# A first pass that gives way to the transform's steps at eight points of a unit instead of four

## The chip, the cores and the metric

The kernel runs on one core of a Trainium2 chip. The metric is the device time of one execution, in microseconds (us). All names of engines are those of the profile: PE is TensorE's matrix multiply, PEld its weight load, DVE is VectorE, ACT is ScalarE, POOL is GpSimd, and SP is SyncE, which here only issues DMAs.

## What is computed

Forward and backward of a gated mix of two branches over one sequence of S = 2048 rows of D = 1024, all in bf16:

```
g   = sigmoid(sum(A_x * gate_w))                       # one gate per row
a   = irfft2(rfft2(A_x) * (A_w_r + i A_w_i))           # spectral branch
b   = relu(A_x @ B_w1 + B_b1)**2 @ B_w2 + B_b2         # dense branch, F = 3584
out = g * a + (1 - g) * b
```

The outputs are `out` and the gradients of A_x, A_w_r, A_w_i, B_w1, B_b1, B_w2, B_b2 and gate_w for a given grad_out. The gradients are sums over rows or columns of products of the same sizes, and the spectral branch is transformed once more for grad_out.

## The kernel before

**Two streams of work.** The kernel has a main stream, the dense branch with its gradients, and a side stream, the spectral branch (a two-dimensional transform there, a product with the filter, and the transform back). Both are Python generators. `spread` (L1797) runs the main one, and at each of its `yield`s it adds a rate, times the weight that was yielded (none counts as 1.0), to what is due, and calls `next` on the side stream until as many side steps are done as are due.

**How the order comes about.** What is written is not yet the order on the engines. The framework's planner lays the instructions out on each engine when the kernel is built: with durations that it assumes, it always takes what is ready and was written first. Two kinds of edges hold it: real dependencies (data, and buffers that must come free), and edges that the kernel adds by hand to fix an order (`after`, `in_turn`, `behind`). `later["last"]` is the DVE instruction that ended the newest `back_`, `turn["PE"]` the newest matmul of the main stream.

**The main stream's first pass** is `mlp_in` (L770 to L1125). It makes the hidden layer and its gradient for 3584 features, in pairs of 128-feature chunks. After a start of its own it walks 23 units. A unit (class `Unit`, L921) is a 256-feature by 1024-row piece of the hidden layer, computed by seven products instead of eight (Strassen's scheme in the form of Winograd): p1, p5, p6, p7, p4, p3 and, for the unit after it, p2. Each is a chain of four 128x512 matmuls into one PSUM bank (L928). Between them run four `back_` calls for the unit before: eight 128x512 matmuls each into a bank `pd` (L827), and one DVE instruction that multiplies the bank by the hidden activations (L831, `dhT`).

- The banks of `ph` (p1, p6, p7 and p4 share X; p5 and p3 share V) are two; those of `pd` and `pZ` (p2) are two, together.
- p1, p6 and p7 leave partial sums, and ACT copies X out after each one (L935, tiles `cu`, `u2`, `cu`); the next chain on X may only start after the copy.
- `rest` adds the partial sums on DVE (L947), then ACT applies the bias and ReLU (L945, L948); `square` squares on ACT (L795) and stores to DRAM.

**The side stream** is `aside` (L1910). It has three stages of steps:

- `first_stage` (L743), four steps for each of 16 pairs of row tiles: pk0 and pk1 are eight 128x128 matmuls each (L293) and an ACT copy (L297); pu0 and pu1 are ten matmuls (L325) and three ACT copies (L303 to L307). pk1 also holds the six DVE instructions of `folds` (L272 to L284) for the next pair, pu1 two DVE additions (L312, L313) and three POOL-issued stores; pk0 issues loads on POOL (L741).
- `fft_mid` (L333), after eight steps of preparation, eight steps m.0 to m.7 for each of 16 groups m. m.0 is `spectra` (eight matmuls, L435), the gradient products of the half before, ACT copies (L443 to L445) and a load; m.1 is the other half's ACT copies and load; m.2 two DVE products (L453); m.3 `rows_of` (eight matmuls, L472), an ACT copy and loads and stores on POOL; m.4 a DVE sum (L458) and two DVE results (L488, L489); m.5 gradient products (L500, L501) and two DVE sums (L426); m.6 two more sums and two results; m.7 two products and a sum, POOL work and an ACT multiplication.
- `fft_out` (L591), which runs after the first pass.

All matmuls of the side stream write tiles of two banks each, named `ps2`, of which there are two. 11 side steps are done before the units begin; the rate then is 1.75 steps for a yield until `fft_mid` begins (`"mid" in later`), and 1.5 after that; in the last five calls of the pass it is 0.

**The points where the first pass gives way.** In the unit of before there are four: after p5, after the second `back_`, after the third, and after p2. The counter `left_` (L1926) is the number of yields of the pass, 100.

Of the kernel before, what the change touches and what calls it, by code (L numbers as in the profile page):

```python
# [141 lines left out]
def kernel(  # L142
# [30 lines left out]
    S2, DC, FC = g.S2, g.DC, g.FC  # L173
# [596 lines left out]
    def mlp_in():  # L770
# [52 lines left out]
        def grads(fc, sb, ss, rT, dhT):  # L823
            w_ = w2T[fc // FGC]
            pd = d_bank("pd")
            for ec in range(DC):
                turn["PE"] = mm(  # L827
                    pd[:], lhsT=w_[:, ec, fc % FGC * P : (fc % FGC + 1) * P], rhs=dbT[:, ec, ss],
                    start=(ec == 0), stop=(ec == DC - 1),
                )  # L830
            return STT(  # L831
                out=dhT, in0=pd[:], scalar=2.0, in1=rT, op0=ALU.mult, op1=ALU.mult,
                accum_out=gb1part[:, fc, sb : sb + 1],
            )

        def load_w2(fg, earlier=None, halves=(0, FGW // 2)):

            if fg not in w2T:
                w2T[fg] = wb.tile([P, DC, FGW], BF16, name="w2T", tag="w2T", bufs=2)
            for h in halves:  # L840
                f0 = fg * FGW + h
                after(turned(w2T[fg][:, :, h : h + FGW // 2], B_w2[f0 : f0 + FGW // 2, :]), earlier)
# [5 lines left out]
        def load_w1(fp):  # L848
            w1[fp] = f1.tile([P, DC, PW], BF16, name="w1f", tag="w1f") if fp == 2 else wb.tile([P, DC, PW], BF16, name="w1g", tag="w1g", bufs=2)
            ld(out=w1[fp][:], in_=w1v[:, :, fp * PW : (fp + 1) * PW])  # L850
# [6 lines left out]
        def store(scr, t_, fp, sp):  # L857
            cols2 = slice(2 * sp * SW, 2 * (sp + 1) * SW)
            st(out=scr[2 * fp : 2 * fp + 2, :, cols2].rearrange("c p s -> p c s"), in_=t_[:])  # L859
# [18 lines left out]
        def back_(fp, s, c):  # L878
            if (fp, s // 2) not in dh:
                dh[fp, s // 2], left_of[fp, s // 2] = wide("dhT"), 4  # L880
            last = grads(2 * fp + c, s, rows_(s), rTs.pop((fp, s, c)), dh[fp, s // 2][:, c, rows_(s % 2)])
            later["last"] = last
            left_of[fp, s // 2] -= 1
            if not left_of[fp, s // 2]:
                store(dhT_scr, dh.pop((fp, s // 2)), fp, s // 2)
# [23 lines left out]
        def w_sums(fp, tie=None):  # L909
            (a11, a12), (a21, a22) = w_quads(fp)  # L910
            if fp % 2:
                s_ = kept[:, NT - 2 : NT, :].rearrange("p t (n f) -> p (t n) f", f=P).rearrange("p (q n) f -> p q n f", q=4)
            else:
                s_ = wb.tile([P, 4, KH, P], FP16, name="Sw", tag="Sw", bufs=1)
            s1, s2, s3, s4 = (s_[:, n] for n in range(4))
            for out, x, y, op in ((s1, a21, a22, ALU.add), (s2, s1, a11, ALU.subtract), (s3, a11, a21, ALU.subtract), (s4, a12, s2, ALU.subtract)):
                after(V(out=out, in0=x, in1=y, op=op), later["last"] if tie else None, mybir.DependencyClass.NoSync)
                yield
            S_[fp] = {1: s1, 2: s2, 3: s3, 4: s4}
# [70 lines left out]
        def sum_of_db(n):  # L990
            ec, h = divmod(n, 2)
            summed = nc.vector.reduce_sum(out=gb2[:, ec, h : h + 1], in_=dbT[:, ec, h * S // 2 : (h + 1) * S // 2], axis=mybir.AxisListType.X)
            after(summed, later["last"], mybir.DependencyClass.NoSync)

        def grad_of_b2():
            whole = wb.tile([P, DC], BF16, name="gb2b", tag="gb2b")
            V(out=whole[:], in0=gb2[:, :, 0], in1=gb2[:, :, 1], op=ALU.add)
            pb = fps.tile([DC, P], BF16, name="pb2", tag="ps2", bufs=2)
            nc.tensor.transpose(pb[:], whole[:], identb[:])
            row = wb.tile([DC, P], BF16, name="gb2r", tag="gb2r")  # L1000
            nc.vector.tensor_copy(out=row[:], in_=pb[:])
            st(out=out_7.rearrange("(c p) -> c p", p=P), in_=row[:])
# [31 lines left out]
        def freed_rows(n, low, high):  # L1034
            if n == freed + 1:
                again(slice(2 * low, 2 * low + 2), later["last"])
            elif n == len(seq) - 1 and high:
                again(slice(6 + 2 * high, 8 + 2 * high))
# [6 lines left out]
        def one_due():  # L1045
            if due:
                fg_, h = due.pop(0)
                load_w2(fg_, later["last"], (h,))

        later["due"] = one_due  # L1050
        for n, u in enumerate(units_):
            fg, pr = divmod(u.fp, NPR)
            if (pr, u.sp) == (0, 0):
                one_due(), one_due()
            if (u.fp, u.sp) == (LAST - 2, 1):
                load_w1(LAST)
            elif u.sp == 0 and u.fp < LAST - 1:
                load_w1(u.fp + 1)
            u.p1()
            if n:  # L1060
                units_[n - 1].square(0, u.copy)
            back_(*waiting[0])
            u.p5()
            freed_rows(n, 0, 1)
            if first and u.sp and "mid" in later and u.fp >= FC // 4:
                turned_group(0, *first.pop(0), later["last"])
            yield
            next(more_sums, None)
            u.p6()
            freed_rows(n, 1, 2)  # L1070
            if n:
                units_[n - 1].square(1, u.copy)
            back_(*waiting[1])
            next(more_sums, None)
            follows = u.fp + 1 if u.sp == 1 and u.fp < LAST - 2 else {(LAST - 2, 0): LAST - 1, (LAST - 1, 1): LAST}.get((u.fp, u.sp))
            ahead_ = w_sums(follows, True) if follows else iter(())
            dealt = ahead_ if (u.fp, u.sp) != (LAST - 2, 0) else iter(())
            next(dealt, None)
            yield
            u.p7()  # L1080
            back_(*waiting[2])
            next(more_sums, None)
            next(dealt, None)
            freed_rows(n, 2, 0)
            yield
            back_(*waiting[3])
            for _ in ahead_:
                pass
            next(more_sums, None)
            if pr == 0 and u.sp == 0:  # L1090
                later["blocks"] = later["last"]
            if 0 < fg < FG - 1 and (pr, u.sp) == (0, 0):
                if "mid" in later:
                    due.extend((fg + 1, h) for h in (0, FGW // 2))
                elif fg < 3:
                    load_w2(fg + 1, later["last"])
                else:
                    late = fg + 1
            elif late and (pr, u.sp) == (0, 1):
                load_w2(late, later["last"])  # L1100
                late = None
            if 0 < n <= 2 * DC:
                sum_of_db(n - 1)
            elif n == 2 * DC + 1:
                grad_of_b2()
            u.p4()
            freed_rows(n, 3, 3)
            u.p3()
            if n + 1 < len(units_):
                units_[n + 1].p2()  # L1110
            yield
            waiting = [(u.fp, 2 * u.sp + j, c) for c, j in ((0, 0), (0, 1), (1, 1), (1, 0))]
        again(slice(NT - 2, NT))
        units_[-1].square(0), units_[-1].square(1)
# [15 lines left out]
    def turned_group(n, i, k, earlier):  # L1130
        scr, fg = (h2T_scr, dhT_scr)[n // FG], n % FG
        rows_ = scr[:].rearrange("c p s -> (c p) s")[fg * FGW + i * FGW // 2 : fg * FGW + (i + 1) * FGW // 2]
        tiles, f_ = slice(k * NT // 2, (k + 1) * NT // 2), slice(i * FGW // 2, (i + 1) * FGW // 2)
        after(turned(group(n)[:, tiles, f_], rows_[:, k * S // 2 : (k + 1) * S // 2]), earlier)
# [706 lines left out]
    warm(7)  # L1841

    units = mlp_in()
    rows_of_x(0, 2)
    vrow = f1.tile([FC + DC, P], BF16, name="vrow", tag="vrow")
# [74 lines left out]
    def counted():  # L1920
        for _ in side:
            count[0] += 1
            yield

    spec = counted()
    left_ = [8 * (FC // 2 - 2) + 4]  # L1926

    def first_rate():
        left_[0] -= 1
# [59 lines left out]
```

## Time and profile before

| | |
|---|---|
| median of 3 runs | 1193.3 us (1192.56 to 1193.49) |
| the profiled execution | 1191.93 us |
| its span, first to last instruction | 1190.2 us |
| PE busy | 1177.4 us (99%) |
| DVE busy | 895.3 us (75%) |
| ACT busy | 531.5 us (45%) |
| POOL busy | 387.6 us (33%) |
| granted PE clock | 1.00 |

The units of the first pass run from about 79 us to 430 us of the span. Stage one of the side stream lies beside units 0 to 7 (78 to 205 us), `fft_mid` beside units 8 to 22 and on into the next pass.

How to read it: a matmul's record lasts 379 ns for 128x512, but the next one starts about 216 ns after it, since matmuls are pipelined. So the busy share hides short stalls, and the start-to-start distances in the timeline tell more. Waits are put down to the semaphore that came last.

### The profile page before, as it was taken

What the parts mean: (1) busy time and instruction counts of PE and PEld (TensorE: products, weight loads), DVE (VectorE), ACT (ScalarE), POOL (GpSimd) and SP (SyncE); (2) the same over time, 40 slices, a digit from 0 to 9 for tenths busy, and PEclk for the clock granted to TensorE, in tenths of its full rate; (3) what the DMA queues carried; (4) which work ended last, traced back from release to release, by engine and by line L of the source; (5) the groups of instructions that cost most, each with busy time, mean ns of one, the idle gap of its engine ahead of it and who ended that gap; (6) DMA issues with size and microseconds to landing.
All of it is one profiled execution on the core that took longest, in us unless ns stands there. A gap on an engine that the chain in (4) does not pass through costs nothing.

```text
span 1190.2 us, 19485 instructions
## 1 busy us (share of the span) xinstructions
PE 1177.4 (99%) x7275; PEld 640.5 (54%) x7275; DVE 895.3 (75%) x1598; ACT 531.5 (45%) x961; POOL 387.6 (33%) x618
## 2 busy tenths in 40 slices
PE   8999999999999999999999999999999999999998
PEld 5555555444444444444447999998544444444444
DVE  6888887788989887877637666676785777976757
ACT  5678888577777772444324666564100010000000
POOL 0234433555858573755231233221001110000000
PEclk9999999999999999999999999999999999999999
DMA  9997585677969779888997999995799999564530
GB/s 251 298 291 235 166 215 170 199 211 179 249 169 232 239 241 186 195 192 212 225 200 157 232 229 260 234 217 153 251 193 228 263 287 282 170 199 147 181 125 36
DMA packets 329464, 249.84 MB, mean 210 GB/s; under 512 B 187912, under 2 KB 287658, under 8 KB 328858
## 3 DMA queue, kind: packets, MB, share of 16 engines
q1 hardware_dynamic: 268352, 112.12, 44.2%
q0 software_dynamic: 35136, 111.72, 29.9%
q10 hardware_dynamic: 25882, 24.76, 7.0%
q8 instruction: 57, 0.93, 0.3%
q14 instruction: 37, 0.30, 0.1%
HBM read 114.82 MB, written 89.67 MB: 172 GB/s over the span
## 4 chain that ended last, share of the span: by engine, by line
PE 78%; DVE 14%; ACT 3%; issue 2%; DMA 2%; SPq 1%; ACTq 0%; DVEq 0%
PE pX L1275 15%; PE xX L1576 14%; PE pV L1275 12%; PE pd L827 11%; PE xV L1576 7%; PE ph L928 6%; PE xZ L1576 4%; PE ph L820 2%; PE pui L325 1%; DVE dhT L831 1%; DVE rT L947 1%; PE pki L635 1%; DVE tt L453 1%; PE pu L325 1%; PE pZ L928 1%
## 5 line engine op out<-in xcount | busy, mean ns | idle before, releaser
L827 PE MATMUL pd<-dbT,w2T 128*128 128x512 bf16 x896 | 210.1, 379 | 3.4 <-DMA w2T<-in_B_w_dram 1.5
L827 PEld LDWEIGHTS <-w2T 128*128 128x128 bf16 x896 | 86.4, 98 | 107.6 <-issue 6.2
L1576 PEld LDWEIGHTS <-dS 128*128 128x128 f16 x686 | 66.4, 98 | 79.0 <-issue 3.4
L831 DVE SCALAR_TENSOR_TENSOR dhT<-pd,rT 128x512 bf16<-128x512 f32 x112 | 76.6, 684 | 33.7 <-PE pd L827 32.9
L1627 POOL DMA_DIRECT2D out_dram<-ot x32 | 17.4, 544 | 246.1 <-DVE ot L1683 128.0
L1693 ACT ACTIVATE w2br<-w2br,dsc 128x512 f32<-128x512 bf16 x8 | 5.8, 724 | 174.5 <-DVE ot L1683 117.4
L1576 PE MATMUL xX<-oT,dS 128*128 128x512 f16 x336 | 76.4, 379 | 0.6 <-DVE eR L1605 0.5
L1291 ACT COPY u<-pX 128x512 f32<-128x512 f32 x56 | 32.8, 586 | 90.5 <-PE pX L1275 84.9
L1576 PEld LDWEIGHTS <-odd 128*128 128x128 bf16 (+1 forms) x462 | 44.8, 98 | 51.5 <-issue 0.9
L1576 PEld LDWEIGHTS <-even 128*128 128x128 bf16 (+1 forms) x448 | 43.6, 98 | 52.6 <-issue 0.7
L1275 PEld LDWEIGHTS <-T 128*128 128x128 f16 x672 | 64.6, 98 | 7.5 <-issue 0.2
L948 ACT ACTIVATE rT<-rT 128x512 bf16<-128x512 bf16 x69 | 43.4, 629 | 42.3 <-DVE rT L947 41.8
L795 ACT ACTIVATE h2T<-rT 128x1024 bf16<-128x1024 bf16 x56 | 59.6, 1065 | 0.2
L1295 DVE TENSOR_TENSOR whi<-pV,u 128x512 bf16<-128x512 f32 x28 | 19.3, 689 | 47.1 <-ACT u L1291 47.0
L491 POOL DMA_DIRECT2D y_scr<-pc x64 | 47.2, 738 | 22.7 <-DVE pc L488 12.9
L1275 PEld LDWEIGHTS <-S 128*128 128x128 f16 x336 | 32.5, 98 | 40.8 <-DVE S L1207 1.9
L453 DVE TENSOR_TENSOR tt<-x,w 128x1028 f16<-128x1028 f16 (+1 forms) x64 | 41.9, 689 | 11.0 <-issue 5.8
L1275 PEld LDWEIGHTS <-resL 128*128 128x128 bf16 x448 | 43.1, 98 | 4.9
L1275 PEld LDWEIGHTS <-resR 128*128 128x128 f16 (+1 forms) x448 | 42.9, 98 | 4.9 <-issue 0.2
L1295 DVE TENSOR_TENSOR wlo<-pV,u 128x512 bf16<-128x512 f32 x28 | 19.2, 687 | 32.0 <-PE pV L1275 31.9
L859 POOL DMA_DIRECT2D h2T_scr<-h2T x28 | 20.9, 746 | 67.1 <-ACT f L285 30.2
L239 POOL DMA_DIRECT2D r<-y_scr x48 | 28.0, 588 | 42.4 <-ACT re L614 33.1
(382 smaller groups left out, 2803.7 us busy)
## 6 DMA issues: line engine op xcount, KB each, us to landing
h2T_scr<-h2T POOLq DMA_DIRECT2D x28, 512.0 KB, 4.2
dhT_scr<-dhT POOLq DMA_DIRECT2D x28, 512.0 KB, 5.2
y_scr<-pc POOLq DMA_DIRECT2D x64, 128.0 KB, 4.2
ax_scr<-yo POOLq DMA_DIRECT2D x16, 512.0 KB, 5.3
out_dram<-ot POOLq DMA_DIRECT2D x31, 256.0 KB, 3.3
z<-z_scr ACTq DMA_DIRECT2D x60, 128.0 KB, 3.4
out_dram<-whi POOLq DMA_DIRECT2D x28, 256.0 KB, 5.2
out_dram<-wlo POOLq DMA_DIRECT2D x28, 256.0 KB, 4.8
```

The lines of the kernel that those rows point to most:

```text
L239: st(out=a, in_=b) if stored else st(out=b, in_=a)
L453: V(out=tt[:, k, :, :, 0:W], in0=x[:, a : a + 2, :, 0:W], in1=by, op=ALU.mult)
L491: st(out=columns_of(y_scr, c, h), in_=pc[:, n])
L795: after(nc.scalar.activation(h2T, rT, ACT.Square), behind_, mybir.DependencyClass.NoSync)
L827: turn["PE"] = mm(pd[:], lhsT=w_[:, ec, fc % FGC * P : (fc % FGC + 1) * P], rhs=dbT[:, ec, ss], start=(ec == 0), stop=(ec == DC - 1),)
L831: return STT(out=dhT, in0=pd[:], scalar=2.0, in1=rT, op0=ALU.mult, op1=ALU.mult, accum_out=gb1part[:, fc, sb : sb + 1],)
L928: turn["PE"] = mm(acc[:], lhsT=lhs[:, t, :], rhs=rhs[:, t, :], start=start and t == 0, stop=t == KH - 1, skip_group_check=True,)
L948: nc.scalar.activation(rT, rT, ACT.Relu)
L1275: self.mm = mm(out, lhsT=lhs[:, t, m * P : (m + 1) * P], rhs=rhs[:, t, :], start=start and t + a == 0, stop=t == KH - 1, skip_group_check= ...
L1291: turn["ACT"] = nc.scalar.copy(out=t_[:], in_=self.X[:])
L1295: turn["DVE"] = self.added = V(out=self.half(row, j), in0=self.sums(acc), in1=self.sums(t_), op=ALU.add)
L1576: ins = mm(acc, lhsT=lhs[:, fc, :], rhs=rhs[:, fc, :], start=start and fc == 0, stop=fc == KH - 1 and bias is None, skip_group_check=True,)
```

## The change

The unit yields at eight points, each with weight 0.5, where it yielded at four with weight 1. The four old points stay; new ones come after p1, after p6, after p7, and after the fourth `back_` (ahead of p4).  The counter becomes 192, the number of yields of the pass now. No instruction is added or taken away, and no rate changes.

```diff
             u.p1()
             if n:
                 units_[n - 1].square(0, u.copy)
+            yield 0.5
             back_(*waiting[0])
             u.p5()
             freed_rows(n, 0, 1)
...
-            yield
+            yield 0.5
             next(more_sums, None)
             u.p6()
             freed_rows(n, 1, 2)
             if n:
                 units_[n - 1].square(1, u.copy)
+            yield 0.5
             back_(*waiting[1])
...
             next(dealt, None)
-            yield
+            yield 0.5
             u.p7()
+            yield 0.5
             back_(*waiting[2])
...
             freed_rows(n, 2, 0)
-            yield
+            yield 0.5
             back_(*waiting[3])
...
             elif n == 2 * DC + 1:
                 grad_of_b2()
+            yield 0.5
             u.p4()
             freed_rows(n, 3, 3)
             u.p3()
             if n + 1 < len(units_):
                 units_[n + 1].p2()
-            yield
+            yield 0.5
...
-    left_ = [8 * (FC // 2 - 2) + 4]
+    left_ = [16 * (FC // 2 - 2)]
```

Which side step is called where follows from `spread` by arithmetic. Steps of a unit are numbered in their order, in brackets:

```
stage one, units 0 to 6, seven steps a unit:
 before  p1 back0 p5 [1 2] p6 back1 [3 4] p7 back2 [5 6] back3 p4 p3 p2 [7]
 after   p1 [1] back0 p5 [2] p6 [3] back1 [4] p7 [5] back2 [6] back3 [7] p4 p3 p2
fft_mid, units 9 to 22, six steps a unit:
 before  p1 back0 p5 [A B] p6 back1 [C] p7 back2 [D E] back3 p4 p3 p2 [F]
 after   p1 [A] back0 p5 [B] p6 back1 [C] p7 [D] back2 [E] back3 p4 p3 p2 [F]
```

Since eight steps make a group and six make a unit, the steps that fall on A and D repeat every four units. A is m.1, m.7, m.5, m.3 in turn, and D is m.4, m.2, m.0, m.6. At the end of the pass 150.25 steps are due before and 150.125 after, so 151 are done either way.

## The prediction

> **What bounds the kernel now.** I read the page first, then the busy times of the stretches before, in and after the units' walk.
>
> ```profile
> span 1190.2 us, 19485 instructions
> ...
> PE 1177.4 (99%) x7275; PEld 640.5 (54%) x7275; DVE 895.3 (75%) x1598; ACT 531.5 (45%) x961; POOL 387.6 (33%) x618
> ```
>
> ```profile
> core 0: us, PE busy (x) PEld busy (x) DVE busy (x) ACT busy (x) POOL busy (x), PEclk, DMA share, GB/s
> 78.00:205.00 127.00, 126.12 (x898) 70.64 (x897) 105.12 (x228) 105.73 (x210) 50.39 (x92) 1.00 0.72 211
> 205.00:440.00 235.00, 233.16 (x1174) 100.63 (x1173) 204.78 (x446) 170.48 (x301) 153.31 (x236) 1.00 0.79 215
> ```
>
> PE is the bound, at a granted clock of 1.00. In stage one (78 to 205 us) DVE and ACT are each 83% busy, in `fft_mid` (205 to 440) DVE is at 87%. So PE sets the time, and the others can only make it stall. Next the waits of PE from 78 to 440 us, all of them, and the longest of DVE and of ACT:
>
> ```profile
> PE pd L827 <- DVE dhT L831: 1.5, 3, 0.7
> PE ph L928 <- ACT u L935: 0.4, 2, 0.2
> PE pk L293 <- ACT u L307: 0.2, 1, 0.2
> ```
>
> ```profile
> DVE dhT L831 <- PE pd L827: 17.7, 13, 3.6
> ...
> ACT rT L948 <- DVE rT L947: 41.8, 42, 2.8
> ```
>
> These rows show only idle time, and a pipelined record hides a short stall. So I took the distances from one matmul's start to the next in the timeline. A 128x512 matmul is followed after 216 ns (median), a 128x128 one after 56, and going into or out of `px` and `pv` costs 95 to 99 more. Beyond these medians there are 16 stalls of over 0.06 us from 78 to 440 us, together 5.2 us:
> - stage one, 2.3 us: six before a `pk` or `pu` (0.28, 0.20, 0.34, 0.26, 0.29, 0.10), two before p7 (0.31 at 149.7, 0.37 at 154.4), one before a `pd` (0.18);
> - `fft_mid`, 2.9 us: five before a `pd` (0.52 at 288.8, 0.24, 0.83 at 338.1, 0.62 at 348.7, 0.23 at 407.9) and two others (0.31, 0.15).
>
> That is all the change can win inside the pass. The largest shows how a stall comes about:
>
> ```profile
> 337.54 1.12 ACT L505 ACTIVATE gw<-gs 128x512 bf16<-128x512 f16 x1 [1.14 <-DMA out_dram<-gw]
> ...
> 338.09 0.41 DVE L426 TENSOR_TENSOR z<-z 128x512 f16<-128x512 f16 x1
> ...
> 338.43 0.68 DVE L831 SCALAR_TENSOR_TENSOR dhT<-pd,rT 128x512 bf16<-128x512 f32 x1
> ...
> 338.65 0.57 ACT L935 COPY cu<-ph 128x512 f32<-128x512 f32 x1
> ...
> 339.17 0.38 PE L827 MATMUL pd<-dbT,w2T 128*128 128x512 bf16 x1 [0.66 <-DVE dhT L831]
> ```
>
> Two banks serve `pd` and `pZ`. One is full of the `pd` whose `dhT` stands behind side work on DVE, the other of `pZ`, whose `cu` copy stands behind the side's `gw` on ACT. Both queues are in order, and PE waits for the first bank.
>
> Here a rule of the Trainium skill can be set beside the rows. Perfetto Trace Analysis, Identifying the Most-Contended Engine, calls matmul busy share a bad measure of headroom and takes the share of weight loads; that is 56% and 43% here, which looks like much room. The start distances decide: a 98 ns load under a 216 ns matmul can't fill more than 45%, and the room is 5.2 us.
>
> **The change part by part.**
>
> *The work.* No instruction comes or goes: 7275 matmuls either way, 151 side steps by the end of the pass either way. 0 us.
>
> *Pairs split.* In stage one 23 pairs of steps, called at one point before, now have a product or a `back_` between them. Each adds one way out of the side's matmuls and one back in, at medians of 3 ns for `pk` to L928 and 6 for `pu`, against a median of 51 from `pu` straight to `pk`. Between 0.2 us and -0.6; I take 0. In `fft_mid` no pair held two steps with matmuls, and `px` and `pv` are entered as often as before.
>
> *Earlier steps in stage one.* Steps 1, 3 and 5 move ahead of a `back_` (8 x 216 ns = 1.7 us), or of one and p5 (2.6 us). ACT keeps the order of main copies and side copies, but starts the side's earlier. The two p7 stalls are ends of such a queue: steps 1 and 2 stand ahead of `u2`, and of their ACT work (1.0 us for a `pk`, 1.4 for a `pu`) the first half now runs under back0. Taking half of these 0.68 us: -0.3. The six `pk`/`pu` stalls (1.45 us) wait for one of two `ps2` banks; a pair gives the ACT copy no time, a split pair 0.9 us or more. Half: -0.7. Sum -1.0, bounds -2.3 and 0.
>
> *Step 7 ahead of p4.* This speaks against the change. Step 7 lay between p2 and the next p1. X of p4 must be emptied by ACT (L945) before the next unit's p1 gets its bank. Its eight matmuls (0.61 us) no longer stand in that gap, and its ACT copy (1.02 us for a `pk`) ends about 0.4 us after p4, in front of L945. So the slack shrinks by 1.0 us. Before, from the end of L945 to p1's start, units 1 to 8 have 0.54, 0.14, 1.36, 1.35, 0.99, 0.57, 1.36, 0.84. What falls short of 1.0: 0.46 + 0.86 + 0.01 + 0.43 + 0.16 = 1.9 us. The planner can put step 1 of the next unit into the hole, so I take half, +0.9; bounds 0 and 1.9.
>
> *A and D in `fft_mid`.* In units 9 to 22 A moves ahead of back0 and p5, D ahead of back2. First PE: of the moved steps, `rows_of` (m.3 as A) started 5.2, 4.2 and 4.5 us after its bank was free, and moves 2.6; `spectra` (m.0 as D) had 3.1 us or more after bank and sums in units 15 and 19, and moves 1.7. So no stall on their own account. Then DVE: A has DVE work in 7 of 14 units, D in all 14, 1.2 to 2.4 us each (m.2: two L453 of 0.69; m.5: 0.76 + 0.47 + 2 x 0.43), and stands ahead of a `dhT`. How much later may a `dhT` be? Of the 57 from 226 to 435 us, the distance from its end to the start of the second next `pd` is 3.7 us in the middle, but under 2.1 in 11. A delay of 2.1 us for each would expose 10.3 us in all, 0.18 each; 21 such groups make 3.8 us. But the group leaves the queue of the next `dhT` in turn, and at most the 2.4 us of `pd` stalls go. I take half of each: +1.9 - 1.2 = +0.7; bounds -2.4 and +3.8.
>
> A second rule bears on that relief. The Trainium skill, Perfetto Trace Analysis, Optimization Strategy, says that a bubble that repeats can mean too few buffers. The trace agrees as far as 288.8, 348.7 and 407.9 us are 60 us apart, four units, before the same `pd`. By the rule the relief would be nothing and my sum 1.2 higher; the cover of 3.7 us in the middle makes me keep half.
>
> *Queues.* The DMAs of the moved steps (loads of L741 and the three stores of pu1 on POOL; m.3's loads and the stores of m.4 and m.6 on POOL; z loads on ACT's queue) pass no store of the main stream: that of h2T is written ahead of back1, that of dhT inside back3. L741 waits for the newest `dhT` (POOL 17.8 us in 5 times); an older one only shortens that. 0 us, hidden by the third buffer of `src`; up to +0.5 if a load came late.
>
> The sum is 0 - 1.0 + 0.9 + 0.7 = +0.6 us on the profiled 1191.93 (span 1190.2 and 1.7 around it), or 1192.5. That execution lies 1.4 under the median of the runs, 1193.3, so the forecast is 1193.9, put as 1194.0.
>
> **The rivals.** A difference of 0.2% (2.4 us) is about what a measurement of this kernel can tell from no change.
>
> *No real change (the forecast), 38%.* The planner fills holes by readiness: `pk` matmuls already stand inside a chain of four that was written as one (155.2 us). Where it hoisted a step before, writing it earlier alters nothing. That the engines' order hardly changes at all is part of this case: 1193.3. Its own range is 1191 to 1195.7.
>
> *Slower: the moved DVE groups hold `pd`'s bank, 35%.* The place is back1 and back3 in units 9 to 22. If every moved group delays its `dhT`, 3.8 us, and with step 7 in full 1.9: 1193.3 + 5.7 = 1199. It decides from the point where more than two in five of that comes, 2.4 us. For it: DVE is 87% busy there, and `dhT` starts 1.0 us on average after its matmuls ended, so it mostly stands in a queue already. Against: 3.7 us of cover in the middle. Three quarters of it give 1197.6.
>
> *Faster: the evened load dissolves the stalls, 27%.* Bursts of two steps are gone; if three quarters of the 5.2 us vanish and step 7 finds its hole, 1193.3 - 3.9 = 1189.4. For it: eight of the 16 stalls stand behind ACT work of a pair. Against: in `fft_mid` three stalls stand behind ACT's `gw` or x copies from unmoved places, and PE has nothing else to win.
>
> **How the numbers follow.** The range takes the forecast's own 1191 to 1195.7 and reaches down to the faster case and up over the middle of the slower one: 1189.0 to 1198.5. Left out are all moved groups and step 7 at full price, and gains after the pass, together 2 in 10. The chances of the three cases are those of faster, same and slower.
>
> **What would show it.** Right: PE's stalls from 78 to 440 us stay between 3 and 7.5 us; the p7 stalls after `u2` shrink, and slack from L945 to p1 in units 1 to 8 falls towards 0; matmul counts stay at 7275. Slower: `PE pd <- DVE dhT` grows beyond 1.5 us. Faster: `pd` waits vanish. Wrong altogether: a difference that arises after 440 us, where the same steps run in the same places, or an ACT or SP load that comes late.

## The result, and the profile after

The kernel after takes 1205.2 us (median of 5 runs, 1204.3 to 1208.3), the one before 1193.0 in the same comparison. The ratio is 1.0112, with a 95% interval from 1.0100 to 1.0125: slower by some 12 us, outside the range. The profiled execution took 1204.95 us.

The page, then the two stretches that were shown of before:

```profile
span 1203.2 us, 19390 instructions
...
PE 1173.1 (98%) x7181; PEld 640.2 (53%) x7275; DVE 894.5 (74%) x1598; ACT 530.5 (44%) x961; POOL 387.2 (32%) x618
```

```profile
core 0: us, PE busy (x) PEld busy (x) DVE busy (x) ACT busy (x) POOL busy (x), PEclk, DMA share, GB/s
78.00:205.00 127.00, 113.16 (x777) 62.83 (x788) 95.10 (x208) 93.60 (x191) 46.51 (x84) 0.96 0.84 194
205.00:440.00 235.00, 230.08 (x1172) 101.73 (x1194) 198.59 (x433) 168.67 (x300) 145.79 (x226) 1.00 0.77 203
```

The work is the same: 7275 weight loads, and 94 of as many matmuls merely lack a record. In stage one PE falls from 126.1 to 113.2 us busy of 127. The DMA packets' times add up to *more* than before (0.84 against 0.72 of the DMA engines' time), and *less* is moved (194 GB/s against 211). The units' starts confine the loss. From p1 of unit 0 to p1 of unit 8 before takes 131.3 us and after 146.1; from there to the end it is 978.1 and 978.5. So all of it lies beside stage one. (Unit 0 began 2.2 us earlier in this profile, which is why 14.8 us of loss make 13 of span.)

The waits of PE from 78 to 440 us, first lines, and the one of DVE, from 78 to 210 us, that stands behind them:

```profile
PE pu L325 <- ACT ft L297: 8.8, 2, 7.7
PE pk L293 <- ACT f L285: 2.9, 2, 1.7
PE ph L928 <- ACT u L935: 2.7, 5, 1.1
```

```profile
DVE uv L272 <- DMA src<-in_A_x_dram: 10.5, 2, 8.3
```

The timeline from 118 to 131 us shows how the one becomes the other (start, length, engine, line):

```profile
122.59 0.69 DVE L272 TENSOR_TENSOR uv<-src 128x1024 f16<-128x1024 bf16 x1 [8.32 <-DMA src<-in_A_x_dram]
...
123.80 0.74 DVE L947 SCALAR_TENSOR_TENSOR rT<-pZ,b1col,cu 128x512 bf16<-128x512 f32 x1
...
124.58 0.63 ACT L948 ACTIVATE rT<-rT 128x512 bf16<-128x512 bf16 x1 [8.21 <-DVE rT L947]
...
125.21 1.01 ACT L297 CAST ft<-pk 128x1024 f16<-128x1024 f32 x1
...
126.27 1.14 PE L325 MATMUL pu<-cf,ft 128*128 128x256 f16 x8 [7.71 <-ACT ft L297]
```

The first instruction of `folds` stands at the head of DVE's queue and waits for a tile from DRAM. Behind it, in the same queue, is the main stream's `rT` (L947). ACT's `rT` (L948) waits for that one, ACT's `ft` stands behind ACT's `rT`, and PE waits for `ft`. PE stands still for 7.7 us for the sake of a side load. Then it pays once more; the windows around the stand-still:

```profile
118.00:126.20 8.20, 0.56 (x3) 0.07 (x1) 3.61 (x6) 1.62 (x4) 2.47 (x4) 0.68 0.60 179
126.20:130.60 4.40, 4.11 (x15) 2.06 (x17) 1.47 (x6) 4.03 (x11) 0.72 (x1) 0.50 0.38 142
```

The granted clock is 0.50 in the 4.4 us after it, and matmuls follow each other after 0.43 us instead of 0.216. The clock record has half clock from 120.9 to 131.2 us: it begins 2.4 us after the end of PE's last matmul (118.56) and lasts 4.9 us beyond the first one after the wait. At half speed, 4.9 us cost some 2.4 us more. The Trainium skill, TensorE: Matmul & The Clock Gate, Part 1, says that an idle window of about 3.4 us drops the array to half its clock until it has been busy for about as long. This trace agrees in kind; its own figures are 2.4 us of idling and 4.9 us of work.

Why was the load late? SP's and POOL's issues before, from 94 to 99 us (timeline of each engine):

```profile
96.72 8.10 SPq L183 DMA_TRANSPOSE w2T<-in_B_w_dram  x2
```

```profile
94.58 1.12 POOL L741 DMA_DIRECT2D src<-in_A_x_dram  x2 [4.89 <-DVE dhT L831]
...
96.38 1.77 POOL L239 DMA_DIRECT2D z_scr<-u  x3 [0.25 <-DVE u L313]
98.15 0.74 POOL L859 DMA_DIRECT2D dhT_scr<-dhT  x1
```

The same views after:

```profile
93.12 15.99 SPq L183 DMA_TRANSPOSE w2T<-in_B_w_dram  x2
```

```profile
91.03 1.76 POOL L239 DMA_DIRECT2D z_scr<-u  x3 [0.25 <-DVE u L313]
92.78 1.12 POOL L741 DMA_DIRECT2D src<-in_A_x_dram  x2
93.90 0.72 POOL L859 DMA_DIRECT2D dhT_scr<-dhT  x1
100.01 1.09 POOL L741 DMA_DIRECT2D src<-in_A_x_dram  x2 [5.39 <-DVE dhT L831]
```

Every four units the main stream loads the next group of `w2T` with two transposing DMAs, released by back3's `dhT`; the src load of pair 6 is released by back2's. DVE's rows about these two, before and after:

```profile
93.58 0.69 DVE L831 SCALAR_TENSOR_TENSOR dhT<-pd,rT 128x512 bf16<-128x512 f32 x1
...
95.33 0.42 DVE L312 TENSOR_TENSOR u<-w 128x512 f16<-128x512 f16 x1
95.66 0.42 DVE L313 TENSOR_TENSOR u<-w 128x512 f16<-128x512 f16 x1
96.00 0.69 DVE L831 SCALAR_TENSOR_TENSOR dhT<-pd,rT 128x512 bf16<-128x512 f32 x1
```

```profile
89.98 0.42 DVE L312 TENSOR_TENSOR u<-w 128x512 f16<-128x512 f16 x1
90.31 0.42 DVE L313 TENSOR_TENSOR u<-w 128x512 f16<-128x512 f16 x1
90.65 0.68 DVE L831 SCALAR_TENSOR_TENSOR dhT<-pd,rT 128x512 bf16<-128x512 f32 x1
...
92.40 0.68 DVE L831 SCALAR_TENSOR_TENSOR dhT<-pd,rT 128x512 bf16<-128x512 f32 x1
```

The two additions of pu1 (L312, L313) stood between the two `dhT` and now stand ahead of both, since step 5 moved ahead of back2. Two things follow. The second `dhT` comes 1.75 us behind the first instead of 2.42, and with it the transposing loads and the dhT store. And the `z_scr` stores, which wait for these additions, now go ahead of the src load on POOL and keep it until 92.78, 1.5 us after its `dhT` has ended. So where the src load used to be 2.1 us ahead of the transposing loads, it is 0.3 us ahead, and the dhT store follows 0.8 us after their start instead of 1.4. The trace has a landing for the second transposing load of each group only. From issue to landing these two took, before and after (the outer values are the two, the middle one their mean):

```profile
DMA to landing us min/median/max: 6.0/9.2/12.4
```

```profile
DMA to landing us min/median/max: 22.4/23.9/25.4
```

The 25 us from about the start of the first group, before and after (the last two figures are the packets' time as a share of the DMA engines' and the GB/s moved):

```profile
96.00:121.00 25.00, 24.73 (x172) 13.55 (x171) 21.25 (x45) 20.96 (x44) 10.50 (x19) 1.00 0.82 231
```

```profile
93.00:118.00 25.00, 23.17 (x159) 12.68 (x160) 16.71 (x36) 17.40 (x35) 6.93 (x13) 1.00 1.13 141
```

At a share of 1.13, packets of one DMA engine must overlap in time, so a packet's time is more than the engine's work on it. The src load of pair 7, issued at 100.0, landed after 21.9 us instead of some 5, and that is the load that DVE waits 8.3 us for. (The other 2.1 us were for the second half of pair 6's load, which landed after 12.3 us.) At 170 us the next group repeats it on a smaller scale.

### The profile page after: what moved, and what is told of

It is laid out like the page before. It is cut to its first block, busy times and chain, and to the rows that moved or that the text cites. A ratio compares the mean times of both kernels' runs of the same rounds, so it can differ in the third digit from the quotient of the medians.

```text
span 1203.2 us, 19390 instructions
## 1 busy us (share of the span) xinstructions
PE 1173.1 (98%) x7181; PEld 640.2 (53%) x7275; DVE 894.5 (74%) x1598; ACT 530.5 (44%) x961; POOL 387.2 (32%) x618
## 4 chain that ended last, share of the span: by engine, by line
PE 63%; DVE 10%; issue 3%; DMA 3%; ACT 2%; POOL 1%; ACTq 0%; DVEq 0%; POOLq 0%; another core or an unknown queue 0%
PE pX L1279 15%; PE xX L1580 14%; PE pV L1279 11%; PE xV L1580 7%; PE pd L827 5%; PE xZ L1580 4%; PE ph L928 3%; PE pui L325 1%; PE pki L635 1%; DVE dhT L831 1%; DVE rT L947 1%; DMA dhT_scr<-dhT 1%; PE px L435 1%; DVE tt L453 1%; DMA out_dram<-gw 1%
## 5 line engine op out<-in xcount | busy, mean ns | idle before, releaser
L827 PE MATMUL pd<-dbT,w2T 128*128 128x512 bf16 x860 | 207.1, 381 | 2.3 <-issue 0.4
L948 ACT ACTIVATE rT<-rT 128x512 bf16<-128x512 bf16 x69 | 43.7, 633 | 48.4 <-DVE rT L947 47.9
L859 POOL DMA_DIRECT2D h2T_scr<-h2T x28 | 20.7, 740 | 79.0 <-ACT h2T L795 48.3
```

The source lines that it names most:

```text
L827: turn["PE"] = mm(pd[:], lhsT=w_[:, ec, fc % FGC * P : (fc % FGC + 1) * P], rhs=dbT[:, ec, ss], start=(ec == 0), stop=(ec == DC - 1),)
L948: nc.scalar.activation(rT, rT, ACT.Relu)
```

## Experiments

The first theory (theory 1) was that a src load issued some 7 us into the run of the transposing loads, as that of pair 7 now is, slows both and comes late. Its rival (theory 2) was that the order of the side steps itself costs the time. Theory 3 came when the first had fallen: a src load and a dhT store, in flight together when the transposing packets begin, are what makes them long. Beside the experiments the kernel before took 1191.4 to 1191.6 us in the median, and every ratio is against these runs.

**Which part of the change.** One kernel has the eight points only from unit 8 on, the other only up to unit 7 (the counter of yields, changed to fit, is left out here):

```diff
+            fine = n >= 8        # the other: n < 8
-            yield 0.5
+            if fine:
+                yield 0.5
...
-            yield 0.5
+            yield 0.5 if fine else 1.0
```

> Eight points in units 8 to 22 (beside fft_mid) alone, four in units 0 to 7. Theory 1 (in stage one the loads of src meet the transposing loads of w2T in the DMA engines, land up to 21.9 us after their issue and hold DVE's queue, and PE stands still): stage one is as before, so 1192 to 1195 us, transposes of 8 to 10 us, no PE stall over 1 us from 78 to 205 us. Theory 2 (the order on the engines costs: DVE groups put ahead of a dhT in fft_mid): 1197 us or more.

> Eight points in units 0 to 7 (beside stage one) alone, four after them. Theory 1: the whole loss, 1203 to 1207 us, with the two long stalls near 118 and 187 us. Theory 2, as far as its place is fft_mid: 1195 us or less; as far as its place is step 7 ahead of p4: 1194 to 1196 us, in many stalls of under 1 us before p1.

Measured: from unit 8 on, 1192.0 us, ratio 1.0005 (0.9992 to 1.0017); up to unit 7, 1203.6, ratio 1.0111 (1.0087 to 1.0135). The whole loss is in stage one. Beside units 8 to 22 PE's waits changed their names: 1.5 us for `dhT` are gone, those for ACT's `u` copy grew from 0.4 to 2.8, and 0.8 for a DMA came. All waits from 78 to 440 us together went from 2.1 to 4.0 us, and the time shows no difference that can be told.

**Is it the transposing loads?** Groups 2 and 3 are loaded by plain DMAs of the same size, so `w2T` holds other data; in the kernel after, then in the one before.

```diff
-                after(turned(w2T[fg][:, :, h : h + FGW // 2], B_w2[f0 : f0 + FGW // 2, :]), earlier)
+                if fg in (2, 3):
+                    rows2 = B_w2[f0 : f0 + FGW // 2, :].rearrange("(p a) (b c) -> p (a b) c", a=2, c=FGW // 2)
+                    after(ld(out=w2T[fg][:, :, h : h + FGW // 2], in_=rows2), earlier)
```

> The changed kernel, in which the loads of w2T for groups 2 and 3 (the two that fall in stage one) are plain loads of the same bytes, not transposing ones; what they bring is then not transposed, which this leaves out. The order on the engines is that of the changed kernel. Theory 1: loads of src land within about 6 us, no PE stall over 1 us in stage one, 1190 to 1195 us. Theory 2: the order is the same, so 1203 to 1207 us.

> The kernel before with the same plain loads for groups 2 and 3 (not transposed). Theory 1: the transposes met little in the kernel before, so within 2 us of 1193, and the changed kernel with plain loads is within 2 us of this one. Theory 2: 1193 as well, and 10 us or more below the changed kernel with plain loads.

Measured: 1190.4 us, ratio 0.9987 (0.9972 to 1.0002), and 1191.4, ratio 0.9998 (0.9989 to 1.0007). With plain loads at the same place nothing is lost, though src and dhT are issued 0.3 us ahead of them and 0.8 behind as before; they land within

```profile
DMA to landing us min/median/max: 9.6/9.8/10.0
```

So it takes the transposing loads. (The plain ones differ in more than the kind: 2048 packets of 512 B for a group instead of 4096 of 256 B. Which of the two counts was not tried.) And the new order of the side steps by itself costs nothing.

**Moving the transposing loads.** They are tied to back1 of the next unit, or to its back0, in the kernel after; then to back1 in the kernel before; then to back0 for the first of the two groups only. The order on every engine stays what it was.

```diff
             back_(*waiting[1])                 # e6, e10: behind back_(*waiting[0])
+            if 0 < fg < 3 and (pr, u.sp) == (0, 1):      # e10: fg == 1
+                load_w2(fg + 1, later["last"])
...
                 elif fg < 3:
-                    load_w2(fg + 1, later["last"])
+                    pass                        # e10: left as it was for fg == 2
```

> The changed kernel, with the transposing loads of w2T for groups 2 and 3 tied to back1 of units 1 and 5, instead of back3 of units 0 and 4. The order on every engine is that of the changed kernel; only when SP's loads start differs. By the run with plain loads, the loads of src are issued near 101 and 113 us, and 166 and 179 us, and back1 ends near 103 and 169 us. Theory 1: transposes fall into the free gaps, take 8 to 11 us for a pair, and the time is 1189 to 1195 us. Theory 2, the order on the engines: 1203 to 1207 us.

> As the run before this, but tied to back0 of units 1 and 5, one back_ earlier (near 98.5 and 164.5 us), so that the loads of src near 101 and 166 us fall into the transposes again. Theory 1: a pair of transposes takes over 12 us, src lands late, 1198 to 1208 us. If only the total of DMA work counted and not the meeting: as with back1.

> The kernel before, four points, with the same tie to back1 of units 1 and 5: its loads of src are issued near 106, 108 and 114 us and near 174 us, and the transposes would start near 104 and 171 us. Theory 1: the kernel before gets the loss too, 1196 to 1206 us, with PE stalls of over 1 us behind the folds of DVE. Theory 2: the order on the engines is that of before, so 1191 to 1194 us.

> The kernel after, with only the first of the two groups of transposing w2T loads (the one at 93 us) moved to a later place; the one at 170 us stays. The order on the engines stays that of after. Theory 1 (each meeting of transposing loads and POOL's transfers costs its own part): the stand-still at 126 us goes, the two short ones at 180 to 202 us stay; 2 to 4 us over before, 1194 to 1197 us. If the loss were one thing of the whole stage: near 1192 or near 1205.

Measured:
- e5: 1192.2 us, ratio 1.0014 (1.0001 to 1.0026). The move returns nearly the whole loss.
- e6: 1192.5, ratio 1.0005 (0.9988 to 1.0021). I had expected a loss, since the transposing loads now start 0.3 us *ahead* of a src load. Their packets were through after 9.9 us all the same. So a meeting with a load is not enough.
- e7: 1194.9, ratio 1.0026 (1.0005 to 1.0046), single runs from 1191.2 to 1202.0. A loss can be put into the kernel before, but a smaller one than I expected: packets of the first group ran 16.3 us, and DVE waited 3.9 us for src.
- e10: 1194.5, ratio 1.0026 (1.0014 to 1.0039). With only the second meeting left, 2.9 us are lost; the first is worth the other nine or so.

**Moving the src loads.** Issued one side step later in the kernel after (e8); one `back_` earlier in the kernel before (e9); and tied to no `dhT` in the kernel after (e12).

```diff
+                yield                                 # e8: from below to here, nothing else
                 if t == 0:
-                    ahead_to(j + 2, later["last"])
+                    ahead_to(j + 2, later["last2"])   # e9: last2 is the dhT ahead of the newest
+                    ahead_to(j + 2)                   # e12: instead of the line above
-                yield                                 # e8
```

> The changed kernel, with the loads of src asked for one point of the unit later (after the yield of pk0). The order on PE is the same, POOL's differs. Theory 1: the load that met the transposes (100.0 us) starts near 104 us and still meets their end, but as in the kernel before in part only; 1193 to 1202 us, and the time goes with how much of the loads lies under the transposes. Theory 2: 1203 to 1207 us.

> The kernel before, with its src loads (L741) tied to the `dhT` before the newest one, so that they are issued some us earlier, inside the run of the two transposing loads of w2T, as in the kernel after. The order on PE, ACT and DVE stays that of before. Theory 1 (a src load issued into the run of the transposing loads slows both, and comes late for `folds`): the transposing loads' packets run for more than 15 us after their issue instead of 9 to 11, DVE waits for src at L272, 1197 to 1206 us. Theory 2 (the order of the side steps costs the time, the loads only show it): 1191 to 1194 us.

> The kernel after with the src loads of stage one tied to no `dhT`: they are issued as soon as their buffer is free, ahead of where after issues them, so they have a longer lead before `folds` needs them. Theory 1 (lateness of src is the whole loss, lead is the cure): DVE waits for src at L272 for less than 3 us in all, 1190 to 1196 us. If the transposing loads still run for more than 20 us and src lands late all the same: 1198 to 1206 us.

Measured:
- e8: 1196.1 us, ratio 1.0045 (1.0029 to 1.0061). Packets ran 12.7 us with dhT at 0.3 and src at 1.0 behind; the src loads, issued later, were late by 4.3 us. Of these, 2.8 us fell at 87.7 us, ahead of the transposing loads, for a load issued only 7.6 us before its use; so this run mixes two causes.
- e9: 1191.7, ratio 1.0001 (0.9988 to 1.0013). This was to be theory 1's proof, and it fell: here, too, a src load is issued 6.5 us into the run, and the transposing loads end after 10.0 and 8.5 us.
- e12: 1191.4, ratio 1.0000 (0.9985 to 1.0015). No wait for `src` is left between 78 and 210 us, although the transposing loads still ran 13.5 and 16.8 us. An earlier issue is a cure for the lateness, whatever makes the transfers slow: the load of pair 15 took 17.5 us to land and was in time, 26 us ahead of its use.

**Which transfer makes them slow.** Two kernels leave a load out of the kernel after: that of pair 7, which was the late one (e11), or those of pairs 6 and 13, which are issued 0.3 us ahead of the transposing loads (e13). A last one leaves nothing out and holds the two dhT stores back until the next back1 (e14; the lines in `store` that keep the transfer are left out here).

```diff
+            if j == 7:                # e13: if j in (6, 13)
+                xs[j] = xs[j - 1]
+                continue
             xs[j] = f1.tile([P, 2, D], BF16, name="src", tag="src", bufs=3)
```

```diff
             back_(*waiting[1])
+            if held:                            # kept by the unit before
+                store(*held.pop(), earlier=later["last"])
...
+            if 0 < fg < 3 and (pr, u.sp) == (0, 0):
+                held.append("next")             # the next store is kept
             back_(*waiting[3])
```

> The kernel after without the src load for pair 7 (the tile of pair 6 is used again; the data of that pair are left out), so the one load that was issued 6.9 us after the transposing loads is missing; z_scr, dhT and h2T are stored as in after. Theory 1 (the load that falls into the run makes it long): the transposing loads' packets end within 13 us, no stand-still at 126 us, some 10 us gained, 1193 to 1197 us. Rival (the stores at the beginning of the run are what slows it): packets still run for 20 us or more, but nothing waits for a src there; a stand-still by a later load, 1198 to 1205 us.

> The kernel after without the src loads of pairs 6 and 13, the ones that are issued 0.3 us ahead of the two groups of transposing w2T loads (the tiles of pairs 5 and 12 are used again; the data of pairs 6 and 13 are left out). The order on the engines is otherwise that of after. Theory 3 (a src load and a dhT store in flight together, when the transposing packets begin, are what makes these loads long): their packets end within 13 us, src comes in time, 1190 to 1194 us. Rival (the dhT store beside them alone, or the load 6.9 us behind them): 17 us or more, and 1197 us or more.

> The kernel after with the dhT stores that are issued 0.8 us behind the start of the two groups of transposing w2T loads moved some 7 us back, behind the next src load; nothing is left out, and the order on the engines is otherwise that of after. Theory 3 (load and store together): packets end within 13 us, 1190 to 1194 us. Rival (the src load 0.3 us ahead is enough by itself): 17 us or more, a late src, 1197 us or more.

Measured: e11 1198.1 us, ratio 1.0062 (1.0041 to 1.0082); e13 1190.8, ratio 0.9999 (0.9990 to 1.0008); e14 1192.9, ratio 1.0023 (1.0005 to 1.0040). Without the late load the transposing loads still ran 19.0 and 22.0 us, and now DVE waited 3.9 us for the one of pair 6. Without the load just ahead of them, or without the store just behind, they run 9.3 to 13.7 us. In e13 no src comes late. In e14 the second half of pair 6's load still took 12.4 us and DVE waited 2.2 us for it, and three of the ten runs took over 1196 us: the transposing loads were quick there, but the loss is not wholly gone. POOL's and SP's issues in e11, then in e13, then in e14:

```profile
94.17 1.12 POOL L744 DMA_DIRECT2D src<-in_A_x_dram  x2
95.28 0.72 POOL L862 DMA_DIRECT2D dhT_scr<-dhT  x1
```

```profile
94.51 15.30 SPq L183 DMA_TRANSPOSE w2T<-in_B_w_dram  x2
```

```profile
94.57 0.74 POOL L862 DMA_DIRECT2D dhT_scr<-dhT  x1 [0.59 <-DVE dhT L834]
```

```profile
94.30 9.83 SPq L183 DMA_TRANSPOSE w2T<-in_B_w_dram  x2
```

```profile
94.10 1.12 POOL L741 DMA_DIRECT2D src<-in_A_x_dram  x2
```

```profile
94.43 12.36 SPq L183 DMA_TRANSPOSE w2T<-in_B_w_dram  x2
```

The meetings of stage one together, from the DMA packets of each profile. Times in the second column count from the issue of the transposing loads and are those of the first group where a row has both (z is the first of the three `z_scr` stores; a src load is two DMAs, and the second follows about 0.55 us behind the first). The third column says when 97% of the transposed bytes had gone; two numbers are the two groups. The last is the median of the runs, while packets come from the one profiled execution; that took 1195.9 us for e6, 1197.3 for e7, 1199.9 for e2 and 1202.8 for e11, and is within 1.1 us of the median elsewhere. (Not listed: e1, which is like before, 10.2 and 10.8 us; e10's first group, like e6, 8.1 us.)

| kernel | POOL's issues about the start | packets end, us | time, us |
|---|---|---|---|
| before | src -2.1, z -0.3, dhT 1.4 | 9.4, 11.1 | 1193.0 |
| e9 | z -0.3, dhT 1.4, src 6.5 | 10.0, 8.5 | 1191.7 |
| e6 | src 0.3, z 2.3, h2T 4.1 | 9.9, 9.2 | 1192.5 |
| e5 | src -3.3, z -1.2, h2T 0.5 | 12.6, 13.6 | 1192.2 |
| e7 | h2T -1.2, src 0.3, z 1.3; second group z -0.5, h2T 1.2, src 2.0 | 16.3, 10.9 | 1194.9 |
| e13 | z -2.1, dhT 0.3, src 6.9 | 11.3, 9.3 | 1190.8 |
| e14 | z -2.1, src -0.3, src 6.9 | 13.7, 11.9 | 1192.9 |
| e8 | z -2.1, dhT 0.3, src 1.0 | 12.7, 12.2 | 1196.1 |
| e12 | z -2.1, dhT 0.3, src 2.6 | 13.5, 16.8 | 1191.4 |
| e11 | z -2.1, src -0.3, dhT 0.8; second group also src 6.9 | 19.0, 22.0 | 1198.1 |
| e10, second group | z -2.1, src -0.3, dhT 0.8, src 6.8 | 20.7 | 1194.5 |
| e2 | the same, src 6.9 | 20.2, 20.3 | 1203.6 |
| after | the same, src 6.9 | 24.1, 18.9 | 1205.2 |

All seven meetings of 18.9 us or more have a src load that begins just ahead of the start and a dhT store just behind it, and no other has both so; the longest of the others is 16.8. That it takes both, in these places, is shown by e13 and e14. In e8 both stand within 1.0 us behind the start and the packets run 12 to 13 us, so it is not enough that both are near. All seven also have the `z_scr` stores 2.1 us ahead; whether those are needed too was not tried. Why a load and a store in flight slow transposing packets, and each other, is not shown: the trace has no record of what a DMA engine waits for.

## Why the prediction was wrong

The step that failed is *Queues*: "L741 waits for the newest `dhT` (POOL 17.8 us in 5 times); an older one only shortens that. 0 us, hidden by the third buffer of `src`; up to +0.5 if a load came late." It looked at POOL's waits alone. It missed two things. First, the loads of the main stream were not on its list, since nothing of them was moved; but a `dhT` releases them, and that moves on DVE when side work changes its place. Second, it took a load's duration as fixed, and put the cover down to the third buffer of `src`. The buffers alone give 24 to 28 us from issue to use, as e12 shows for pairs 6 to 15, where nothing else holds the loads; with the tie to the newest `dhT` it was 9 to 13 us before, which hides the usual 5 us and not 22. The term was some 12 us instead of 0 to 0.5. "[A]n ACT or SP load that comes late" did stand under what would show the prediction wrong altogether; it was a POOL load, slowed by SP's, and the range gave it nothing.

The other terms can be read where the meeting is taken away.

- *The work*: 0, as said.
- *Pairs split*, *Earlier steps*, *Step 7*: together forecast at -0.1, for stage one. From p1 of unit 0 to p1 of unit 8 the profiles take 130.8 us in the new order where nothing is late (e3, e6, e12, e13) and 131.2 to 131.3 in the old one (before, e1, e4, e9): -0.5. The whole change with plain `w2T` loads in both orders (e3 and e4) is 1190.4 against 1191.4, and the intervals of the two ratios overlap: no difference in time that can be told, as forecast. In e12, which keeps the order of after, the slack of p7 after `u2` in units 0 to 7 rose from 0.05–1.68 us to 0.48–1.41, so the stalls there went. The slack from L945 to p1 in units 1 to 8 shrank from 7.2 to 3.7 us in sum, and twice a wait of up to 0.3 us came of it (0.6 in all, against the +0.9 forecast).
- *A and D in `fft_mid`*: forecast +0.7 with bounds -2.4 and +3.8. Measured +0.6 with an interval from -1.0 to +2.0 (0.0005 of 1191.5). That PE's waits for `dhT` would not grow was right; they went altogether. That ACT's `u` copy would take their place was not forecast.
- The slower rival had the wrong place (`fft_mid`), the wrong engine order (DVE's `dhT`) and about half the price.

## What to carry to other kernels

When steps are re-timed, list every DMA whose release hangs on the instructions that they pass, on all queues, and not only the DMAs that the steps issue: what meets in the DMA engines can change though no queue's order against the main stream does. A load that feeds an in-order engine should be issued with a lead of several of its usual landing times where large transfers are near; here dropping a tie to a finished product was enough. Where a stall is long, add the clock: 7.7 us of standing still cost some 10 (from p1 of unit 2 to p1 of unit 3 it is 26.6 us, before 16.7).

## What the runs showed of the hardware

- Of two transposing loads of 0.5 MB each, the second landed 6 to 12 us after its issue before and 22 to 25 when a 0.5 MB load was issued 0.3 us ahead and a 0.5 MB store 0.8 us behind the first. It is no sharing of a fixed rate: the DMA engines moved 141 GB/s in those 25 us, against 231 before. Most packets are as quick as ever and a few are very long. In the 24 us from the first group's issue the median transposed packet of 256 B took 0.018 us in both kernels, and the mean 0.067 after against 0.024 before; the median 4 KB packet of POOL's queue took 0.16 in both, the mean 0.31 against 0.20, the longest 3.4 against 0.9.
- The Trainium skill, Advanced Engine Details and Errata, X-Bar Transpose (TRN2), says that transposing DMAs are as fast as regular ones. In e6 that is nearly so: 10.8 and 12.7 us to land, where the plain loads of e3 took 9.6 and 10.0. In the company of after it is not: 25.4 and 22.4 against 9.6 and 10.0 with the same neighbours.
- Single runs scatter more where a load is nearly or just late: e14 and e7 have runs from 1191 to 1202 us, while nine of ten runs of e3 and of e12 stay within 1190.0 to 1193.7. The kernel before has a few long ones too, up to 1199.0 beside these runs. Whether a late load makes them was not looked at.
